# Raw k and v of three pairs of batches in 1-MB loads, and raw rows in weight buffers that are still empty: retention and a top-2 mixture of experts on one core

## The chip, the core and the metric

The kernel runs on one core of a Trainium2 chip. The metric is the device time of one execution in microseconds (us); before the change its median is 443.01 us over 3 runs (438.04, 443.01 and 443.7).

The core has five engines with a queue of instructions each, which they work off in order: PE (matmuls; PEld is its weight load, which overlaps), DVE, ACT, POOL and SP. SP only issues loads and stores (DMAs); POOL issues those that gather, scatter or convert, beside its own work. An instruction that waits holds up what stands behind it in its queue.

## What is computed

The inputs q, k and v have 8 batches, 8 heads, 576 positions and head size 64, in float32. The reference, cut:

```python
scores = (1/8) * q @ k^T
ret = scores * Dmat            # Dmat[h, i, j] = gamma_h ** (i - j) where i >= j, else 0
attn = ret @ v                 # (8, 8, 576, 64)
x = attn.transpose(0, 2, 1, 3).reshape(4608, 512)
logits = x @ w_gate + log1p(exp(x @ w_noise)) * noise    # (4608, 8)
# the two best experts of each row, softmax over the two:
out[row] += weight * (relu(x[row] @ w1[e]) @ w2[e])      # w1[e] 512 x 1024, w2[e] 1024 x 512
```

## The kernel before, in words

**Units.** The attention part handles the batches in four pairs (bp = 0 to 3). A pair has four units u = 4 bp to 4 bp + 3: its two batches, each in two halves of four heads. `unit` (L430) gives pair, half (hq) and batch of u. A unit covers the first 512 positions; the last 64 of all heads of a pair form a "tail" (`load_tail` L464, `tail` L643).

**Raw rows.** `load` (L437) brings a unit's rows to the chip: q in a tile of 128 x 1024 float32 (two loads of 256 KB, one for each pair of heads), k and v in two such tiles each (c = 0 and 1, 256 positions each). The k and v tiles hold all 8 heads of one batch, so they serve two units: units 0 and 1 load their four heads each (256 KB a load), and from unit 2 on the first unit of a batch loads both halves (512 KB a load). In a k or v load each partition gets 512 bytes per head in one piece, in a q load 2 KB. All these tiles come from a class of 10 buffers, "big", which the experts' weights use later too.

**What happens to them.** `cast` (L475) converts a unit's raw rows to bfloat16 in "half" buffers: k on ACT or DVE (L489, L491), q on POOL or DVE with a table of decays (L498), v likewise (L505). `tr` transposes k and q on PE (L527, L521), `scores` (L552) and `states` (L585) multiply, `out_` (L620, L630) writes the unit's rows, transposed, to a tile xT of the pair.

**Routing.** When a pair is done, `route` (L711) computes the gates (PE L734), the two best experts and the ranks of the rows in them (DVE and POOL, many small operations; PE L798, L800), a table of rows per expert (PE L851), and writes the rows, transposed back (PE L874), with their weights and targets, from "xg" buffers to a buffer xd in memory (SP L883).

**Experts.** A tile of an expert gathers up to 128 rows per block from xd (POOL L1007, indirect), transposes them (PE L1029), multiplies by w1 (L1083 in pairs of blocks early on, L1109 with up to four blocks later) and w2 (L1171, L1181), and stores to or adds to rows in memory (SP L1229, POOL L1203 and L1238). The early pairs of blocks, of experts 0 to 2, start while attention still runs (`CLOSE`, L34: how many rows of each expert are worked on after each pair of batches). The three weight buffers W0 to W2 (128 x 8192 bfloat16) are filled for these experts by converting loads that POOL issues (`weights`, L932; L940 and L944, four of 512 KB each as stored), the later experts' through "big" (L954, L957) and casts to W. W0 is loaded once unit 10's rows have landed, W1 and W2 once unit 15's have (`WAIT`, L31).

**The order.** `record` (L1248) lists all operations with a priority (the unit, or 100 and more for experts); a planner, `Plan.run` (L114), then walks through them with estimated costs, and picks each time what can start first on an engine, by when its inputs, a buffer of its class and the engine are free. Where two engines are given for an operation it picks one. What comes out is a fixed order of instructions for each of the five queues. So another cost, another buffer or another transfer anywhere moves instructions in all queues. Estimated landing: 0.24 us per head for a k or v load, 0.72 for a q load. There are 8 semaphores for SP's loads, so that a load waits until the eighth before it has landed.

Of the kernel before, what the change touches and what calls it, by code (L numbers as in the profile page):

```python
# [8 lines left out]
F32 = mybir.dt.float32  # L9
F16 = mybir.dt.float16  # L10
BF16 = mybir.dt.bfloat16
# [6 lines left out]
P = 128  # L18
N = 4608
NCOL = N // P  # L20
E = 8
F = 1024
DM = 512
KD = DM // P
KF = F // P
# [219 lines left out]
class Kernel:  # L245
    def __init__(self, tc, ctx, src, gates, noise, w1, w2, out, xd, yd):
        self.tc, self.nc = tc, tc.nc
        self.src, self.gates, self.noise, self.w1, self.w2, self.out = src, gates, noise, w1, w2, out
        self.xd, self.yd = xd, yd
        nc = self.nc  # L250
        self.pl = pl = Plan()
        self.cp = ctx.enter_context(tc.tile_pool(name="fix", bufs=1))
        self.ps = ctx.enter_context(tc.tile_pool(name="ps", bufs=1, space=bass.MemoryType.PSUM))
        mk = lambda n, k, sh, dt: [(self.cp.tile(sh, dt, name=f"{n}{i}"), None) for i in range(k)]
        pl.cls("big", mk("big", 10, [P, 1024], F32), exp=4, xt=3, rt=1)
        pl.cls("half", mk("half", 21, [P, 512], F32), cs=9, exp=15, xt=3, tl=6, rt=1)
# [175 lines left out]

    def inp(self, fn, t, prio, dma):

        self.inps.append(self.pl.op("SP", 0.55, fn, w=[t], prio=prio, dma=dma, after=self.inps[-5:-4]))

    def load(self, u):  # L437
        pl, nc = self.pl, self.nc
        bp, hq, b = self.unit(u)
        d = self.u[u] = {}  # L440

        if not hq:
            self.raw = {n: [pl.buf("big", "att") for c in range(2)] for n in "kv"}
        for n in "kqv":
            if n == "q":
                t = d["rawq"] = pl.buf("big", "att")
                s = self.src[n][2 * bp + b, 4 * hq:4 * hq + 4]

                for a in range(2):
                    self.inp(lambda e, s=s, t=t, a=a: nc.sync.dma_start(  # L450
                        out=t.t[a::2].rearrange("p (h x) -> p h x", h=2),
                        in_=s[2 * a:2 * a + 2, :512].rearrange("h (p r) d -> p h (r d)", r=8)), (t, a), u, 0.72)
                continue
            d["raw" + n] = self.raw[n]
            if hq and u > 1:
                continue
            h0, nh = (4 * hq, 4) if u < 2 else (0, E)
            for c, t in enumerate(self.raw[n]):
                self.inp(lambda e, n=n, t=t, c=c: nc.sync.dma_start(
                    out=t.t[:, h0 * P:(h0 + nh) * P].rearrange("p (h x) -> p h x", h=nh),  # L460
                    in_=self.src[n][2 * bp + b, h0:h0 + nh, 256 * c:256 * c + 256].rearrange("h (p r) d -> p h (r d)", r=2)),
                    (t, hq) if u < 2 else t, u, 0.24 * nh)

    def load_tail(self, bp, prio):  # L464
        pl, nc = self.pl, self.nc
        d = self.tails[bp] = {}
        for n in "kqv":
            t = d["raw" + n] = pl.buf("half", "tl")
            for b in range(2):
                self.inp(lambda e, n=n, t=t, b=b: nc.sync.dma_start(  # L470
                    out=t.t[b * HD:(b + 1) * HD].rearrange("p (h d) -> p h d", h=E),
                    in_=self.src[n][2 * bp + b, :, 512:, :].rearrange("h s d -> s h d")),
                    (t, b), prio, 0.8)

    def cast(self, u):  # L475
        pl, nc = self.pl, self.nc
        d = self.u[u]
        hq = self.unit(u)[1]
        hs = slice(4 * hq, 4 * hq + 4)
        tab, tabq = self.fixed["tab"], self.fixed["tabq"]  # L480
        bf = lambda b: b.t.bitcast(BF16)
        kn, qb, vn = (pl.buf("half", "cs") for _ in range(3))
        rk, rq, rv = d.pop("rawk"), d.pop("rawq"), d.pop("rawv")

        def k(e, c):
            i = rk[c].t.rearrange("p (g h r d) -> p g h r d", g=2, h=4, r=2)[:, hq]
            o = bf(kn).rearrange("p (r c h d) -> p c h r d", r=2, c=2, h=4)[:, c]
            if e == "ACT":
                nc.scalar.activation(o, i, Act.Copy, scale=0.125)  # L489
            elif e == "DVE":  # L490
                nc.vector.tensor_scalar_mul(o, i, 0.125)  # L491
        for c in range(2):
            pl.op({"ACT": 0.63, "DVE": 0.43}, 0, lambda e, c=c: k(e, c), r=[(rk[c], hq)], w=[(kn, c)], prio=u, port=True)

        def q(e):
            i = rq.t.rearrange("p (h r d) -> p h r d", h=2, r=8)
            o = bf(qb).rearrange("p (r h d) -> p h r d", r=8, h=2)
            self.eng(e).tensor_tensor(o, i, tabq.t[:, 2 * hq:2 * hq + 2].unsqueeze(3).to_broadcast([P, 2, 8, HD]), Alu.mult)  # L498
        pl.op({"DVE": 1.23, "POOL": 1.91} if u > 1 else {"DVE": 1.23}, 0, q, r=[rq, tabq], w=[qb], prio=u, port=True)

        def v(e, c):
            i = rv[c].t.rearrange("p (g h r d) -> p g h r d", g=2, h=4, r=2)[:, hq]
            o = bf(vn).rearrange("p (r c h d) -> p c h r d", r=2, c=2, h=4)[:, c]
            t = tab.t[:, hs, 2 * c:2 * c + 2].unsqueeze(3).to_broadcast([P, 4, 2, HD])
            self.eng(e).tensor_tensor(o, i, t, Alu.mult)  # L505
        for c in range(2):
            pl.op({"DVE": 0.69, "POOL": 1.06}, 0, lambda e, c=c: v(e, c), r=[(rv[c], hq), tab], w=[(vn, c)], prio=u, port=True)
        d.update(kn=kn, qb=qb, vn=vn)

    def tr(self, u):  # L510
# [737 lines left out]
    def record(self):  # L1248
        pl = self.pl
# [7 lines left out]
        for u in range(NU + 1):  # L1257
            bp = u // 4
# [29 lines left out]
        self.ne = ne = len([t for t in ts if t[2] < 3])  # L1288
        landed = lambda u: [o for o in pl.ops if o.dma and o.prio == u]
        for e, u in enumerate(WAIT):  # L1290
            self.weights(e, 40 + e, True, landed(u))

        ahead = 2
        fetched = 0
        for i, t in enumerate(ts[:ne]):
# [5 lines left out]
            g = self.down(i, t)  # L1301
            for k in range(KF):
                r, w, c = g.deps(k)
# [4 lines left out]
        for i in range(ne, len(ts) + 1):  # L1308
# [4 lines left out]
            if i < len(ts):  # L1313
                e = ts[i][0]
# [8 lines left out]
            else:  # L1323
                e, po, hT = ts[-1][0], self.t[i - 1]["po"], self.t[i - 1]["hT"]
                for s in range(len(po)):
                    def last(_, s=s):
# [3 lines left out]
                        else:  # L1330
# [3 lines left out]
                          r=[(hT[f // 2], f) for f in range(KF)] + [(self.W[e], KD + f) for f in range(4)], w=[po[s]], prio=pr)  # L1334
# [164 lines left out]
```

## Time and profile before

| what | us |
|---|---|
| median of three runs | 443.01 |
| span of the profiled execution, first to last instruction | 439.4 |
| PE busy | 381.7 |
| POOL busy | 282.1 |
| ACT busy | 248.1 |
| DVE busy | 181.6 |

Of the profiled execution itself the record gives the span; it lies between the lowest and the median of the three times. A line of the profile gives the line of the kernel (L505 is line 505), the engine, the operation, the tiles (written <- read, buffer numbers left out) and how often. "[2.46 <-POOL half L498]" says that the engine stood idle for 2.46 us ahead of it and that POOL's work at line 498, which wrote a "half" buffer, ended the wait. "PEclk" is the share of PE's full clock that was granted; it is 1 or 0.5 at any moment. The share of the 16 DMA engines can exceed 1, since packets overlap.

### The profile page before, as it was taken

How to read it: one execution, taken by the hardware profiler on the slowest of the kernel's cores; microseconds unless marked ns; L12 is line 12 of the kernel's file. 1: busy time of each engine (PE TensorE's matmuls, PEld its weight loads, DVE VectorE, ACT ScalarE, POOL GpSimd, SP SyncE). 2: the span in 40 equal slices, each digit the busy share in tenths (PEclk: the TensorE clock that was granted, in tenths of full speed). 3: DMA queues.
4: the chain of work that ended last, by engine and by line, in shares of the span. 5: the costliest groups of instructions: out<-in, count | busy, mean ns of one | idle time of the engine just before them, and what ended most of it. 6: DMA issues, size and time to landing. Idle time of an engine off the chain costs nothing. (4 is left out here: it accounts for less than half of the span.)

```text
span 439.4 us, 11274 instructions
## 1 busy us (share of the span) xinstructions
PE 381.7 (87%) x4352; PEld 242.1 (55%) x4352; DVE 181.6 (41%) x501; ACT 248.1 (56%) x422; POOL 282.1 (64%) x363
## 2 busy tenths in 40 slices
PE   2787676778899859999999999999999997999990
PEld 1576566667677646765566544545544543454450
DVE  4744488784378665202243452143123211222231
ACT  5688586777776646657656647464446332434320
POOL 8774788795889526553447766666676562777544
PEclk9999698679999988999999999999999998999996
DMA  8997999999996999548499996996999999765524
GB/s 244 310 263 160 303 267 262 304 277 264 277 264 108 218 211 264 169 143 278 127 354 375 362 384 192 328 339 167 311 365 133 168 147 267 202 209 189 165 75 145
DMA packets 98235, 105.36 MB, mean 240 GB/s; under 512 B 31711, under 2 KB 72160, under 8 KB 98179
## 3 DMA queue, kind: packets, MB, share of 16 engines
q1 hardware_dynamic: 82914, 67.72, 52.6%
q0 software_dynamic: 15264, 36.89, 34.3%
q8 instruction: 35, 0.57, 0.6%
q14 instruction: 22, 0.17, 0.1%
HBM read 83.20 MB, written 26.63 MB: 250 GB/s over the span
## 5 line engine op out<-in xcount | busy, mean ns | idle before, releaser
L1171 PE MATMUL ps<-W,half 128*128 128x512 bf16 x576 | 189.1, 384 | 4.8 <-ACT half L1092 2.8
L1109 PE MATMUL ps<-big,W 128*128 128x512 bf16 (+4 forms) x640 | 182.1, 330 | 0.7 <-ACT half L1092 0.7
L1092 ACT ACTIVATE half<-ps 128x512 bf16<-128x512 f32 (+5 forms) x181 | 90.3, 506 | 106.6 <-PE ps L1109 88.8
L1007 POOL DMA_INDIRECT xg<-xd,xi x80 | 84.1, 1052 | 69.3 <-issue 17.9
L1171 PEld LDWEIGHTS <-half 128*128 128x128 bf16 x576 | 56.1, 99 | 67.6 <-issue 5.2
L1109 PEld LDWEIGHTS <-W 128*128 128x128 bf16 x640 | 62.8, 98 | 47.6 <-issue 1.7
L1233 DVE SCALAR_TENSOR_TENSOR half<-ps,xg,half 128x512 f32<-128x512 f32 (+1 forms) x46 | 30.4, 667 | 68.6 <-PE ps L1171 49.1
L1238 POOL DMA_INDIRECT out_dram<-half,xg x39 | 38.8, 994 | 23.4 <-DVE half L1233 8.9
L560 DVE TENSOR_TENSOR half<-ps,mask 128x512 bf16<-128x512 f32 x64 | 40.5, 682 | 20.8 <-PE ps L552 17.7
L1203 POOL DMA_INDIRECT half<-yd,xg x39 | 39.4, 1010 | 11.9 <-issue 10.4
L279 ACT ACTIVATE half<-ps 128x1024 bf16<-128x1024 bf16 (+1 forms) x35 | 34.4, 1002 | 6.5 <-PE ps L521 2.7
L505 POOL TENSOR_TENSOR half<-big,tab 128x512 bf16<-128x512 f32 x32 | 33.5, 1060 | 3.7 <-DMA big<-in_v_dram 3.5
L1083 PE MATMUL ps<-half,W 128*128 128x256 bf16 (+1 forms) x288 | 29.6, 258 | 5.6 <-ACT xg L279 3.9
L498 POOL TENSOR_TENSOR half<-big,tabq 128x1024 bf16<-128x1024 f32 x14 | 26.6, 1902 | 8.0 <-DMA big<-in_q_dram 5.5
L1083 PEld LDWEIGHTS <-W 128*128 128x128 bf16 x288 | 24.3, 99 | 9.4 <-issue 6.4
L279 ACT ACTIVATE tb<-ps 64x512 bf16<-64x512 f32 x32 | 18.9, 591 | 18.5 <-PE ps L585 17.3
L279 ACT ACTIVATE W<-big 128x1024 bf16<-128x1024 f32 x23 | 23.9, 1052 | 7.6 <-DMA big<-in_moe_w_dram 6.8
L1233 DVE SCALAR_TENSOR_TENSOR half<-ps,gm,half 128x512 f32<-128x512 f32 x6 | 4.5, 751 | 52.9 <-ACT half L1223 29.6
L1223 ACT ACTIVATE half<-ps,xg 128x512 f32<-128x512 f32 x28 | 19.1, 685 | 9.6 <-PE ps L1171 8.5
L279 ACT ACTIVATE xT<-ps 128x512 bf16<-128x512 f32 (+1 forms) x40 | 19.9, 555 | 6.2 <-PE ps L701 4.7
L279 ACT ACTIVATE xg<-ps 128x1024 bf16<-128x1024 bf16 (+1 forms) x19 | 17.1, 934 | 7.4 <-DMA xd<-xg 7.3
L489 ACT ACTIVATE half<-big 128x512 bf16<-128x512 f32 x29 | 17.6, 633 | 5.5 <-DMA big<-in_k_dram 5.4
(189 smaller groups left out, 445.6 us busy)
## 6 DMA issues: line engine op xcount, KB each, us to landing
big<-in_moe_w_dram SPq DMA_DIRECT2D x40, 512.0 KB, 8.9
yd<-half SPq DMA_DIRECT2D x41, 256.0 KB, 7.7
big<-in_q_dram SPq DMA_DIRECT2D x32, 256.0 KB, 8.7
big<-in_k_dram SPq DMA_DIRECT2D x14, 512.0 KB, 6.3
big<-in_v_dram SPq DMA_DIRECT2D x14, 512.0 KB, 9.8
W<-in_moe_w_dram POOLq DMA_DIRECT2D x12, 512.0 KB, 9.2
xd<-xg SPq DMA_DIRECT2D x16, 264.0 KB, 6.4
xg<-xd,xi POOLq DMA_INDIRECT x80, 5.9
```

The source lines that it names most:

```text
L279: self.nc.scalar.activation(out, in_, Act.Copy)
L498: self.eng(e).tensor_tensor(o, i, tabq.t[:, 2 * hq:2 * hq + 2].unsqueeze(3).to_broadcast([P, 2, 8, HD]), Alu.mult)
L505: self.eng(e).tensor_tensor(o, i, t, Alu.mult)
L560: nc.vector.tensor_tensor(S.t.bitcast(BF16).rearrange("p (h c x) -> p h c x", h=2, c=2)[:, h], p[h].t.rearrange("p (c x) -> p c x", c=2), ...
L1007: ins = nc.gpsimd.indirect_dma_start(out=x.t[:n, :], out_offset=None, in_=self.xd[:rows, :], in_offset=IOff(ap=xi.t[:n, h:h + 1], axis=0), ...
L1083: nc.tensor.matmul(pv()[:, f2, :], lhsT=w.t[:, o:o + P], rhs=xv()[:, di, :n], start=(di == 0), stop=(di == KD - 1))
L1092: self.nc.scalar.activation(o, i, Act.Relu)
L1109: self.mm = nc.tensor.matmul(p.t[:, :n], lhsT=w.t[:, o:o + P], rhs=xv()[:, di, :n], start=(di == 0), stop=(di == KD - 1))
L1171: self.mm = self.nc.tensor.matmul(po.t, lhsT=hv[:, c:c + P], rhs=self.W[e].t[:, o:o + DM], start=(f == 0), stop=(f == KF - 1))
L1203: pl.op("POOL", 1.3, lambda _, b=b, iy=iy, n=self.size(j): nc.gpsimd.indirect_dma_start(out=b.t[:n, :], out_offset=None, in_=self.yd[:rows ...
L1233: pl.op("DVE", 0.75 if n == P else 0.86, lambda _, o=o, b=b, po=po, g=g, n=n: [nc.vector.scalar_tensor_tensor(o.t[:n, c], x, g()[:n], b.t[ ...
L1238: ins = nc.gpsimd.indirect_dma_start(out=self.out[:, :], out_offset=IOff(ap=io()[:n], axis=0), in_=o.t[:n, :], in_offset=None, bounds_chec ...
```

## The change

- Units 0 to 2: as before, 256 KB per load for units 0 and 1 and 512 KB for unit 2; but the tiles now hold both batches of the pair (16 groups of 64 columns by 2 positions, 128 x 2048 float32), so that `cast` picks one of four quarters of a tile (x4) instead of one of two halves.
- Pairs 1 to 3: k and v come once per pair, at its first unit, in two loads of 1 MB each (both batches and all heads of 256 positions).
- Where they lie: those of pairs 0 and 2 in the weight buffers W1 and W2, which hold four such tiles (class "wkv"); those of pairs 1 and 3 in "big", whose ten buffers are now five adjoining pairs.
- q of units 0 to 7 lies in W0, which holds four q tiles (class "wq"); from unit 8 on in "big".
- W0 may be loaded, beside the old condition, once all raw q in it are cast, W1 and W2 once all raw k and v in them are.
- The planner's estimate of a k or v load is 0.22 us per group of 64 columns by 2 positions instead of 0.24.

The core of the diff:

```diff
-        pl.cls("big", mk("big", 10, [P, 1024], F32), exp=4, xt=3, rt=1)
+        bs = [self.cp.tile([P, 2, 1024], F32, name=f"big{i}") for i in range(5)]
+        pl.cls("big", [(x[:, i, :], x) for x in bs for i in range(2)], exp=4, xt=3, rt=1)
...
-        pl.cls("W", mk("W", 3, [P, KD * F + KF * DM], BF16))
+        ws = [self.cp.tile([P, KD * F + KF * DM], BF16, name=f"W{i}") for i in range(3)]
+        pl.cls("W", [(x, None) for x in ws])
+        part = lambda x, i, n: x[:, 2 * i * n:2 * i * n + 2 * n].bitcast(F32)
+        pl.cls("wkv", [(part(x, i, 2048), None) for x in ws[1:] for i in range(2)])
+        pl.cls("wq", [(part(ws[0], i, 1024), None) for i in range(4)])
...
     def load(self, u):
...
-        if not hq:
-            self.raw = {n: [pl.buf("big", "att") for c in range(2)] for n in "kv"}
+        if u % 4 == 0:
+            self.raw = {n: [pl.buf("big", "att", 2) if bp % 2 else pl.buf("wkv", "att") for c in range(2)] for n in "kv"}
...
-                t = d["rawq"] = pl.buf("big", "att")
+                t = d["rawq"] = pl.buf("wq", "att") if u < 8 else pl.buf("big", "att")
...
-            if hq and u > 1:
+            if bp and u % 4 or u == 3:
                 continue
-            h0, nh = (4 * hq, 4) if u < 2 else (0, E)
+            m = slice(0, 2 * E) if bp else slice(4 * u, (4, 8, 16)[u])
             for c, t in enumerate(self.raw[n]):
-                self.inp(lambda e, n=n, t=t, c=c: nc.sync.dma_start(
-                    out=t.t[:, h0 * P:(h0 + nh) * P].rearrange("p (h x) -> p h x", h=nh),
-                    in_=self.src[n][2 * bp + b, h0:h0 + nh, 256 * c:256 * c + 256].rearrange("h (p r) d -> p h (r d)", r=2)),
-                    (t, hq) if u < 2 else t, u, 0.24 * nh)
+                w = [t] if bp else [(t, x) for x in range(m.start // 4, m.stop // 4)]
+                self.inp(lambda e, n=n, t=t, c=c, m=m, bp=bp: nc.sync.dma_start(
+                    out=rows(t, m),
+                    in_=self.src[n][2 * bp:2 * bp + 2].rearrange("b h s d -> (b h) s d")[
+                        m, 256 * c:256 * c + 256].rearrange("h (p r) d -> p h (r d)", r=2)),
+                    w, u, 0.22 * (m.stop - m.start))
...
         def k(e, c):
-            i = rk[c].t.rearrange("p (g h r d) -> p g h r d", g=2, h=4, r=2)[:, hq]
+            i = flat(rk[c]).rearrange("p (g h r d) -> p g h r d", g=4, h=4, r=2)[:, x4]
...
         for e, u in enumerate(WAIT):
-            self.weights(e, 40 + e, True, landed(u))
+            raw = (("wkv", "att"), ("wq", "att"))[e == 0]
+            self.weights(e, 40 + e, True, landed(u) + [o for b in pl.fifo[raw] for o in b.ops])
```

The casts of v and the sources of the tails change in the same way as those of k; `rows` and `flat` give the view of a tile in one piece.

More of the change, by code (lines that the diff above doesn't have):

```diff
@@ L433, in inp @@
     def inp(self, fn, t, prio, dma):
[L435 removed]
+        self.inps.append(self.pl.op("SP", 0.55, fn, w=t, prio=prio, dma=dma, after=self.inps[-5:-4]))
     def load(self, u):
@@ L492, in cast @@
         for c in range(2):
-            pl.op({"ACT": 0.63, "DVE": 0.43}, 0, lambda e, c=c: k(e, c), r=[(rk[c], hq)], w=[(kn, c)], prio=u, port=True)
+            pl.op({"ACT": 0.63, "DVE": 0.43}, 0, lambda e, c=c: k(e, c), r=[(rk[c], x4)], w=[(kn, c)], prio=u, port=True)
         def q(e):
@@ L506, in cast @@
         for c in range(2):
-            pl.op({"DVE": 0.69, "POOL": 1.06}, 0, lambda e, c=c: v(e, c), r=[(rv[c], hq), tab], w=[(vn, c)], prio=u, port=True)
+            pl.op({"DVE": 0.69, "POOL": 1.06}, 0, lambda e, c=c: v(e, c), r=[(rv[c], x4), tab], w=[(vn, c)], prio=u, port=True)
         d.update(kn=kn, qb=qb, vn=vn)
```

12 lines of the change are left out of this document (8 added, 4 removed).

## The prediction

> **What bounds the kernel now.** I read the windows first, with the span cut at the ends of its stages: 0 to 140 us holds the sixteen attention units, 140 to 175 the last two routings, and from 175 on only expert work is left. The columns are the stretch, its length, busy time (and instructions) of PE, PEld, DVE, ACT and POOL, the granted PE clock, the DMA engines' share, and GB/s.
>
> ```profile
> 0.00:45.00 45.00, 28.37 (x672) 23.85 (x672) 23.70 (x128) 31.22 (x46) 30.37 (x67) 1.00 0.92 241
> 45.00:90.00 45.00, 32.96 (x824) 28.02 (x826) 33.38 (x82) 32.20 (x56) 36.40 (x48) 0.81 1.05 285
> 90.00:140.00 50.00, 43.02 (x908) 33.98 (x901) 30.88 (x72) 37.05 (x62) 40.38 (x57) 0.93 0.99 247
> 140.00:175.00 35.00, 27.94 (x354) 20.46 (x354) 21.96 (x84) 20.19 (x37) 18.21 (x39) 0.90 1.00 216
> 175.00:439.00 264.00, 249.43 (x1608) 135.84 (x1606) 71.72 (x138) 127.39 (x224) 156.74 (x155) 0.98 0.80 234
> ```
>
> After 175 us PE is busy 249.43 of 264 us, so that part is PE's own work and the change leaves that work alone. Ahead of it PE stands idle 16.6 us (to 45), 12.0 (to 90), 7.0 (to 140) and 7.1 (to 175), 42.7 in all. The same PE work has to be done before and after, so what the change can win is a part of these 42.7 us, and a microsecond by which an attention unit comes earlier is worth a microsecond only if PE has nothing less to do in that time. In the stage that matters, 45 to 140, POOL is the busiest: 76.8 of 95 us.
>
> Next I looked at the DMA: three windows of ten microseconds, then the issues (transfers of each kind, KB each, median us from issue to landing).
>
> ```profile
> 10.00:20.00 10.00, 7.68 (x149) 6.67 (x149) 7.68 (x22) 6.01 (x10) 6.76 (x25) 1.00 1.13 314
> 30.00:40.00 10.00, 7.95 (x269) 7.04 (x261) 6.96 (x12) 9.54 (x16) 5.85 (x7) 1.00 0.90 178
> 60.00:70.00 10.00, 8.13 (x250) 6.85 (x248) 9.04 (x25) 8.15 (x15) 8.72 (x17) 1.00 0.93 224
> ```
>
> ```profile
> big<-in_q_dram SPq DMA_DIRECT2D x32, 256.0 KB, 8.7
> big<-in_k_dram SPq DMA_DIRECT2D x14, 512.0 KB, 6.3
> big<-in_v_dram SPq DMA_DIRECT2D x14, 512.0 KB, 9.8
> ...
> big<-in_v_dram SPq DMA_DIRECT2D x4, 256.0 KB, 4.3
> ```
>
> Loads run at 314 GB/s when the queue is full and fall to 178 and 224 GB/s in the two stretches in which the small tail loads are issued: 1.36 MB and 0.90 MB not moved, 7.2 us at 314 GB/s.
>
> Third, who waits for raw rows. These lines are the raw buffers' own view from 0 to 140 us: casts by engine with shortest, median and longest ns, and then the idle time of the casting engines by the kind of load that ended it.
>
> ```profile
> L505 POOL TENSOR_TENSOR half<-big,tab x32: 1037/1047/1479, 8.9 to 136.4; 128x512 bf16<-128x512 f32 x32
> L489 ACT ACTIVATE half<-big x29: 613/630/652, 4.2 to 129.2; 128x512 bf16<-128x512 f32 x29
> ...
> L498 POOL TENSOR_TENSOR half<-big,tabq x14: 1895/1902/1926, 19.8 to 130.5; 128x1024 bf16<-128x1024 f32 x14
> ...
>   DMA big<-in_q_dram: 6.9, 4
>   DMA big<-in_k_dram: 5.4, 3
>   DMA big<-in_v_dram: 3.5, 4
> ```
>
> Only 15.8 us of waiting in eleven waits, the first loads of the run among them. So the loads don't hold the casts up much directly. They do it through the order written into each queue: the planner places a cast where it expects its rows. On PE and POOL (start, duration, what, and the idle time before it) that looks so:
>
> ```profile
> 46.30 1.03 PE L521 MATMUL ps<-ident__69,half 128*128 128x128 bf16 x8 [2.46 <-POOL half L498]
> ...
> 92.56 0.51 PE L527 MATMUL ps<-ident__69,half 128*128 128x128 bf16 x6 [2.11 <-ACT half L489]
> ...
> 138.79 0.23 PE L585 MATMUL ps<-half,half 64*64 64x64 bf16 x4
> ...
> 154.63 0.59 PE L1171 MATMUL ps<-W,half 128*128 128x512 bf16 x2 [1.91 <-DMA W<-in_moe_w_dram]
> ```
>
> ```profile
> 35.20 1.05 POOL L505 TENSOR_TENSOR half<-big,tab 128x512 bf16<-128x512 f32 x1 [1.62 <-DMA big<-in_v_dram]
> ...
> 82.10 1.74 POOL L940 DMA_DIRECT2D W<-in_moe_w_dram  x2
> 86.79 1.14 POOL L1007 DMA_INDIRECT xg<-xd,xi  x1 [2.95 <-DVE scr L756]
> ...
> 94.42 1.56 POOL L1007 DMA_INDIRECT xg<-xd,xi  x1 [0.30 <-issue]
> ...
> 104.80 1.05 POOL L505 TENSOR_TENSOR half<-big,tab 128x512 bf16<-128x512 f32 x1 [1.21 <-DMA big<-in_v_dram]
> 111.27 1.11 POOL L1007 DMA_INDIRECT xg<-xd,xi  x1 [5.42 <-DVE half L560]
> ```
>
> The last states matmuls of unit 15 are at 138.79. POOL gathers (L1007) and W0's loads (L940) stand between q and v casts and hold them up.
>
> **The change part by part.** Transfers: k and v take 36 issues now (4 and 14 each); the changed kernel has 24, since each of the last three pairs takes four of 1 MB instead of eight of 512 KB. Bytes and rows of 512 B stay. At 314 GB/s with an engine share of 1.13 the engines have no gap between transfers that a merger could close, so the direct gain is 0; twelve SP issues less are hidden behind the full queue.
>
> Pairs' first units: unit 4 now needs its v behind 1 MB more of k and 1 MB more of v, 2.1 MB or 6.8 us at 314 GB/s; against that the dip to 178 GB/s is filled. Its second v cast, at 35.20, comes 2 to 7 us later, I take 4. Behind it PE waited 2.46 us for unit 5's q anyway, and q5 still follows the tails, so I count between 3 us lost and nothing. Units 6 to 8 then have their k and v at hand; POOL's 8.6 us without work from 45 to 90 bound what that gives, and I take 2. Together 1 us earlier, between 3 later and 4 earlier.
>
> Order on POOL around units 9 and 10: by the built programs W0's first two loads now stand ahead of q9, not behind v10. W0's buffer may be filled once the raw q of units 0 to 7 are cast, which is long past. That costs units 9 and 10 up to 1.74 us, and nothing from unit 11 on, whose casts stand behind these loads in both orders.
>
> Units 11 and 12: both gathers (1.14, and 1.56 after 0.30) go from ahead of unit 11's casts to between q12 and v12. Unit 11 gains their 3.0 us; from v12 on only the wait ahead of them counts, 2.95 us, of which I take half, since the routing's next small operation on POOL needs DVE too. The wait of 1.21 us at 104.80 for v12, and PE's of 2.11 us at 92.56 for a k cast, go, as those rows now lie there. For v12 and all that follows 1.5 + 1.2 = 2.7 us, bounds 0 and 4.2.
>
> Units 13 to 15: ahead of the last v cast the changed POOL has three gathers less (five for eight, 1.11 each), one weights load (0.87), one q cast (1.90) and one half of a v cast (1.05) less, 7.1 us; q13 and that half go to DVE, which is busy 30.88 of 50 us there. The wait of 5.42 us stays, since such a gather is still ahead of q14 and q15. Bounds 2 and 8, taken 7.1. Unit 15 so ends 1 + 2.7 + 7.1 = 10.8 us earlier, at 128; the bounds add up to 1 later and 16 earlier.
>
> What is given back: the planner puts less expert work into that time. Ahead of unit 15's last states the old order has 64 up (L1083) and 30 down matmuls (L1171), the new one 32 and 12.
>
> ```profile
> L1171 PE MATMUL ps<-W,half 128*128 128x512 bf16 x56 | 15.6, 415 | 1.9 <-DMA W<-in_moe_w_dram 1.9
> ...
> L1083 PE MATMUL ps<-half,W 128*128 128x256 bf16 x101 | 12.6, 272 | 1.7 <-ACT half L279 1.2 <-DVE half L281 0.5
> ```
>
> Busy time over count is 0.125 us for an up and 0.279 us for a down matmul (0 to 170 us, slow clock included): 32 x 0.125 + 18 x 0.279 = 9.0 us of PE work moves behind unit 15. PE's idle time falls by 10.8 - 9.0 = 1.8 us only. To that comes the clock: 0.93 over 90 to 140 is half speed for 7 us, begun after the wait at 92.56; without it up to 3 us of PE time, I take 1.5.
>
> Behind unit 15: up to the last table the difference shrinks to 24 up and 8 down, 5.2 us, so PE has work while the two routings run, one after the other through the same DVE tiles. W1 and W2 are loaded once their raw rows are cast and unit 15's rows have landed, which is earlier; their loads still follow the last casts on POOL. The wait of 1.91 us at 154.63 may become 0 or 4 us; I take no change.
>
> Sum: 1.8 + 1.5 = 3.3 us less, a span of 436.1 instead of 439.4. The profiled span is 3.6 us under the median of the three runs shown, 443.01 (438.04 to 443.7), so against the median I forecast 439.7, rounded to 440.
>
> A rule that speaks for much more: four k and v transfers of 256 KB landed after 4.3 us, k's of 512 KB after 6.3, so a line through both has 2.3 us that don't grow with size, and twelve transfers less would be 27 us if the queue paid them one after another. The Trainium skill, "DMA: Bandwidth & Descriptors" (Anatomy of one DMA; Bandwidth) says the same: about 2.0 us fixed per DMA, and batch to 1 MiB or more; by its figure 24 us, an estimate. The windows at 314 GB/s show the fixed part overlapped, and the same page's rules for authors have it overlap where DMAs are issued early.
>
> **Rivals.** (A) The sum above, 436 to 442 us: 0.43.
>
> (B) The loads, not POOL, space the units. Then filling the dips gives the whole 7.2 us, and units without stalls keep PE's clock up: 0.81 over 45 to 90 is half speed for 17 us, about 8 us of PE time, of which I allow 5. 443 - 12 = 431 (429 to 433). For it: the two dips. Against it: POOL's 36.4 of 45 us. 0.22.
>
> (C) Nothing moves: rows lie there earlier, and the casts still wait for their place in POOL's queue and for the `half` buffers that they write. 443 (442 to 446). For it: only 15.8 us of waits for rows. 0.18.
>
> (D) Slower. The 1-MB v of the last pair goes into buffers that hold raw q of units 8 to 11, so its second transfer can't be issued before q11 is cast (after the gather at 86.79 now), and behind it on SP stand the writes of routed rows that the gathers and so q14 wait for. With 9.8 us to landing of a 512-KB v, it decides once q11 is cast later than about 92 us; then units 12 to 15 slip by up to those 9.8 us, and the time is 453. 0.13.
>
> (E) The 2.3 us that don't grow with size are paid twelve times in series, on the path: 443 - 27 = 416. For it: the two medians. Against it: the windows at 314 GB/s. 0.04. By the figure of the Trainium skill, "DMA: Bandwidth & Descriptors", it would be 419, an estimate.
>
> **How the numbers follow.** 440 is A's. Faster by over 2% (under 434.1; 2% is about what a measurement of this kernel can tell from no change) is 0.20 of B, E and 0.02 of A: 0.26. Slower by over 2% (above 451.9) is 0.12 of D and 0.01 of C: 0.13. The rest is 0.61. A range of 429 to 450 leaves out E, the lowest 0.03 of B and 0.12 of D.
>
> **What would show it.** Right: the last L585 at 124 to 130 us instead of 139; PE idle ahead of 175 us near 40 us, more of it saved ahead of 140 than lost behind; more L1083 and L1171 behind the last states; the GB/s at 30 to 40 us well above 178. Wrong: the last L585 at 136 or later (then C or, with SP waiting on the v of unit 12, D), PE idle for over 10 us between unit 15 and the last table (then the routings are what counts), or PE idle under 33 us with the clock near 1.00 from 45 us on (then B).

## The result, and the profile after

The changed kernel takes 458.7 us (median of 4 runs, 457.62 to 464.37), the kernel before 441.95 on the same chip (4 runs, 438.04 to 443.7): a ratio of 1.056, 95% interval 1.038 to 1.074. It is slower, and outside the range of 429 to 450 us. Medians and ranges here are of all runs; ratios and their intervals leave out disturbed executions, so a ratio can differ a little from the quotient of two medians.

The profiled execution took 459.39 us, its span is 457.8. The changed kernel's lines that are named here stand 8 to 12 further down than before: loads of k and v L459 -> L468, of q L450 -> L458, of tails L470 -> L480, casts of q and v L498 and L505 -> L510 and L517, transposes L521 -> L533, states L585 -> L597, writes to xd L883 -> L895, the wide matmuls L1109 -> L1121. The changed kernel's windows by stage, in the columns of the prediction's first fence:

```profile
0.00:45.00 45.00, 25.36 (x526) 20.84 (x528) 21.91 (x118) 27.04 (x40) 27.17 (x69) 0.89 0.96 258
45.00:90.00 45.00, 29.89 (x730) 26.16 (x727) 26.48 (x56) 27.29 (x45) 30.99 (x44) 0.80 0.89 229
90.00:140.00 50.00, 34.10 (x670) 29.20 (x670) 35.43 (x67) 30.18 (x48) 29.55 (x41) 0.73 0.84 220
140.00:175.00 35.00, 31.62 (x686) 24.38 (x685) 27.00 (x87) 22.14 (x42) 26.09 (x46) 1.00 0.87 182
```

PE now idles 19.6, 15.1, 15.9 and 3.4 us in the four stages, 54.0 ahead of 175 us where it was 42.7, and between 90 and 140 the granted clock fell from 0.93 to 0.73. The loads slowed down with it, 220 GB/s there for 247. In the two windows around the first pair's tails, still of the changed kernel:

```profile
30.00:40.00 10.00, 7.00 (x176) 5.80 (x169) 3.27 (x7) 6.73 (x11) 2.75 (x2) 0.77 0.93 244
40.00:50.00 10.00, 5.98 (x124) 5.28 (x117) 3.09 (x5) 4.09 (x8) 3.90 (x7) 0.55 0.77 152
```

The dip is not gone, it has moved. Between 20 and 60 us the poorest ten microseconds of the changed kernel are those at 40 to 50, with 152 GB/s; in the kernel before they are at 32 to 42 us, with 137 GB/s:

```profile
32.00:42.00 10.00, 7.68 (x223) 6.77 (x224) 5.24 (x10) 8.65 (x14) 5.29 (x8) 1.00 0.78 137
```

SP's queue tells why. First the kernel before (start, duration, loads issued), then the changed one:

```profile
40.12 1.28 SPq L450 DMA_DIRECT2D big<-in_q_dram  x2
...
58.90 3.91 SPq L470 DMA_DIRECT2D half<-in_k_dram  x2
...
99.29 6.36 SPq L883 DMA_DIRECT2D xd<-xg  x5
...
108.82 2.21 SPq L450 DMA_DIRECT2D big<-in_q_dram  x2
```

```profile
31.38 1.06 SPq L468 DMA_DIRECT2D big<-in_v_dram  x1
...
35.05 0.71 SPq L468 DMA_DIRECT2D big<-in_v_dram  x1
35.88 2.86 SPq L480 DMA_DIRECT2D half<-in_k_dram  x1
...
47.55 1.28 SPq L458 DMA_DIRECT2D W<-in_q_dram  x2
...
69.67 4.40 SPq L480 DMA_DIRECT2D half<-in_k_dram  x2
...
114.16 2.31 SPq L480 DMA_DIRECT2D half<-in_q_dram  x1
122.95 3.39 SPq L895 DMA_DIRECT2D xd<-xg  x5
126.39 1.29 SPq L458 DMA_DIRECT2D big<-in_q_dram  x2
```

The four lines of the kernel before are unit 5's q, the first tail load of pair 1, the writes of pair 1's routed rows and, behind them, unit 13's q. In the changed kernel the same four are at 47.55, 69.67, 122.95 and 126.39: later by 7.4, 10.8, 23.7 and 17.6 us. The first step is easy to see: k and v of the pair's second batch, 2 MB that nobody needs before unit 6, now stand ahead of eleven small loads (the tails and the noise, 35.88 to 46.90 us), and behind all of them stands the q that unit 5 needs. SP comes to the first of the eleven 6.4 us later than before (35.88 for 29.50), about the time of 2.1 MB at 314 GB/s, 6.7 us. The eleven themselves, of 8 to 128 KB, take SP 11.0 us here and 10.0 us in the kernel before, about 1 us each; in both kernels the dip lies there and just behind.

What the casts wait for: POOL's timeline of the changed kernel.

```profile
34.57 1.90 POOL L510 TENSOR_TENSOR half<-W,tabq 128x1024 bf16<-128x1024 f32 x1 [5.85 <-DMA W<-in_q_dram]
39.15 1.05 POOL L517 TENSOR_TENSOR half<-big,tab 128x512 bf16<-128x512 f32 x1 [2.68 <-DMA big<-in_v_dram]
43.53 1.05 POOL L517 TENSOR_TENSOR half<-big,tab 128x512 bf16<-128x512 f32 x1 [3.33 <-DMA big<-in_v_dram]
52.10 1.90 POOL L510 TENSOR_TENSOR half<-W,tabq 128x1024 bf16<-128x1024 f32 x1 [1.85 <-DMA W<-in_q_dram]
```

Unit 4's second v cast is at 43.53 (35.20 before), unit 5's q cast at 52.10 (before, PE's wait at 46.30 ended with it). And PE:

```profile
44.63 1.20 PE L597 MATMUL ps<-half,half 128*64 128x64 bf16 x24 [3.85 <-POOL half L517]
...
94.95 0.75 PE L709 MATMUL ps<-half,half 64*64 64x64 bf16 x16 [8.13 <-DVE half L696]
...
139.15 0.62 PE L533 MATMUL ps<-ident__69,half 128*128 128x128 bf16 x8 [2.81 <-DVE half L510]
...
152.57 0.23 PE L597 MATMUL ps<-half,half 64*64 64x64 bf16 x4
...
221.12 4.14 PE L1121 MATMUL ps<-big,W 128*128 128x448 bf16 x21
...
250.54 0.32 PE L1121 MATMUL ps<-big,W 128*128 128x192 bf16 x1 [5.93 <-ACT half L1104]
```

The last states of unit 15 are at 152.57 instead of 138.79. The first wide matmul of the experts starts at 221.12; before the change it is this row:

```profile
200.97 6.38 PE L1109 MATMUL ps<-big,W 128*128 128x448 bf16 x33
```

So 20.2 us are lost ahead of it, more than the 18.4 by which the span grew. Up to unit 15 the loss grows in jumps, and a part is made up in between. The start of the q transposes of units 4, 5, 8, 9, 12, 13 and 15 is (before, after): 33.1 and 36.5, 46.3 and 54.1, 65.3 and 75.1, 77.7 and 96.0, 105.3 and 116.7, 119.0 and 139.2, 133.4 and 149.2.

The jump at unit 9 has a cause of its own, which the prediction did not foresee. A cast of 30 columns on DVE, the list of rows for the gathers, in the changed kernel's DVE timeline, and POOL's timeline of the same time:

```profile
86.10 8.47 DVE L875 CAST xi<-L 128x30 int32<-128x30 f32 x1
94.48 0.74 DVE L696 TENSOR_TENSOR half<-ps,maskt 128x256 bf16<-128x256 f32 x2
```

```profile
85.74 1.07 POOL L669 TENSOR_TENSOR half<-half,tab 128x512 bf16<-128x512 f32 x1
86.76 1.91 POOL L510 TENSOR_TENSOR half<-big,tabq 128x1024 bf16<-128x1024 f32 x1
88.61 2.04 POOL L517 TENSOR_TENSOR half<-W,tab 128x512 bf16<-128x512 f32 x2
90.62 1.89 POOL L510 TENSOR_TENSOR half<-big,tabq 128x1024 bf16<-128x1024 f32 x1
92.48 2.04 POOL L517 TENSOR_TENSOR half<-W,tab 128x512 bf16<-128x512 f32 x2
```

The cast took 8.47 us, until POOL's last cast in a row was done; in the kernel before it took 0.29. The next work in DVE's queue is what PE waited 8.13 us for at 94.95.

The jump at unit 13 has a cause on DVE, too. Its q is cast there now:

```profile
134.28 0.69 DVE L1106 TENSOR_SCALAR half<-ps 128x512 bf16<-128x512 f32 x1 [6.44 <-PE ps L1095]
134.89 4.20 DVE L510 TENSOR_TENSOR half<-big,tabq 128x1024 bf16<-128x1024 f32 x1
```

The cast stands behind a step of an early expert (L1106), for which DVE waited 6.44 us, and then takes 4.20 us beside POOL's work from 134.08 to 138.00. On DVE it took 1.21 and 1.22 us in the first units. It is what PE waits 2.81 us for at 139.15. This q was asked for at 126.39 and 127.06, and loads of its kind landed after a median of 4.4 us, so by that estimate it lay there at about 131.5: the order in DVE's queue, not the load, ended the wait.

### The profile page after: what moved, and what is told of

The parts are those of the page before. It is cut to its first block, busy times and chain, and to the rows that moved or that the text cites. A ratio compares the mean times of both kernels' runs of the same rounds, so it can differ in the third digit from the quotient of the medians.

```text
span 457.8 us, 11254 instructions
## 1 busy us (share of the span) xinstructions
PE 387.2 (85%) x4352; PEld 248.3 (54%) x4352; DVE 193.4 (42%) x499; ACT 246.3 (54%) x420; POOL 279.8 (61%) x367
## 5 line engine op out<-in xcount | busy, mean ns | idle before, releaser
L1121 PE MATMUL ps<-big,W 128*128 128x512 bf16 (+4 forms) x640 | 181.6, 330 | 5.9 <-ACT half L1104 5.9
L1104 ACT ACTIVATE half<-ps 128x512 bf16<-128x512 f32 (+5 forms) x181 | 89.3, 498 | 109.3 <-PE ps L1121 97.4
L1121 PEld LDWEIGHTS <-W 128*128 128x128 bf16 x640 | 62.9, 98 | 47.8 <-issue 0.9
L284 ACT ACTIVATE half<-ps 128x1024 bf16<-128x1024 bf16 (+1 forms) x31 | 31.1, 1015 | 14.3 <-PE ps L533 5.0
L1235 ACT ACTIVATE half<-ps,xg 128x512 f32<-128x512 f32 x32 | 21.9, 684 | 16.5 <-PE ps L1183 16.4
L284 ACT ACTIVATE W<-big 128x1024 bf16<-128x1024 f32 x22 | 22.3, 1051 | 7.7 <-DMA big<-in_moe_w_dram 7.5
L597 PE MATMUL ps<-half,half 64*64 64x64 bf16 (+2 forms) x512 | 20.0, 231 | 7.0 <-POOL half L517 3.8
L533 PE MATMUL ps<-ident__69,half 128*128 128x128 bf16 x128 | 13.3, 266 | 12.5 <-POOL half L510 4.7
L597 PEld LDWEIGHTS <-half 64*64 64x64 bf16 (+1 forms) x512 | 17.2, 125 | 10.4 <-issue 8.4
L564 PE MATMUL ps<-half,half 64*64 64x128 bf16 x512 | 13.5, 256 | 9.4 <-ACT half L284 8.5
```

The source lines that it names most:

```text
L284: self.nc.scalar.activation(out, in_, Act.Copy)
L597: nc.tensor.matmul(o[h * HD:(h + 1) * HD, hp, n, :], lhsT=kk[:k, r, c, y], rhs=vv[:k, r, c, y].unsqueeze(1).to_broadcast([k, n.stop - n.st ...
L1104: self.nc.scalar.activation(o, i, Act.Relu)
L1121: self.mm = nc.tensor.matmul(p.t[:, :n], lhsT=w.t[:, o:o + P], rhs=xv()[:, di, :n], start=(di == 0), stop=(di == KD - 1))
L1235: nc.scalar.activation(y.t[:n, c], x, Act.Copy, scale=g()[:n])
```

## The experiments

Sixteen runs were made, in four groups, each group on one chip with runs of the kernel before. In the first group the kernel before itself took 463.74 us, so its times are compared within the group only; the changed kernel was not run there. A dash means that the record has no ratio. One thing limits all of these but e2: an edit to the loads or the estimate makes the planner order all queues anew, so that none of them changes SP's queue alone. POOL's order, for one, differs from the changed kernel's from 45 us on in e8 and from 60 us on in e5.

| run | what it is | us, median (range) | before, there | ratio and interval |
|---|---|---|---|---|
| e1 | after, k and v in 512 KB, batch by batch | 450.75 (447.01-455.24) | 463.74 (456.35-469.48) | - |
| e2 | after, one cast reads PSUM | 475.98 (470.47-478.05) | same | 1.032 (0.996-1.068) |
| e3 | after, estimate 0.30 | 473.37 (467.02-477.44) | same | 1.025 (0.989-1.060) |
| e4 | before, estimate 0.22 | 452.86 (445.34-456.74) | same | 0.987 (0.951-1.024) |
| c_after | after | 458.35 (452.24-462.9) | 442.33 (438.0-444.84) | 1.038 (1.030-1.047) |
| e5 | after's place, 512 KB | 457.68 (451.01-463.12) | same | - |
| e6 | pair 1 as in e1, pairs 2 and 3 in 1 MB | 446.84 (442.56-450.51) | same | 1.009 (1.003-1.014) |
| e7 | pair 1 in 1 MB, the others as in e1 | 463.84 (456.18-467.16) | same | - |
| e8 | after, tails of pair 0 behind q5 | 448.32 (448.0-451.49) | 443.07 (439.43-447.69) | 1.013 (1.005-1.020) |
| e9 | before, tails of pair 0 behind q5 | 441.16 (436.07-442.81) | same | 0.988 (0.978-0.997) |
| e10 | e1 again | 433.64 (432.21-443.5) | same | 0.978 (0.972-0.983) |
| e11 | e1, tails of pair 0 behind q5 | 447.2 (438.42-451.86) | same | 0.996 (0.989-1.002) |
| e12 | e1, estimate 0.24 | 440.96 (433.51-447.45) | 443.18 (431.74-445.65) | - |
| e13 | e1 again | 433.85 (430.58-435.0) | same | - |
| e14 | e4 again | 441.27 (439.62-443.22) | same | - |
| e15 | after | 454.88 (453.11-455.32) | same | - |

**The joint loads undone, everything else kept (e1, e10, e13), and the whole change beside it (e15).** The edit to the changed kernel; every load of k or v is then 512 KB or less and is asked for with the first unit of its own batch:

```diff
-            if bp and u % 4 or u == 3:
+            if u % 2 and u > 1:
                 continue
-            m = slice(0, 2 * E) if bp else slice(4 * u, (4, 8, 16)[u])
+            m = slice(4 * (u % 4), 4 * (u % 4) + (8 if u > 1 else 4))
             for c, t in enumerate(self.raw[n]):
-                w = [t] if bp else [(t, x) for x in range(m.start // 4, m.stop // 4)]
+                w = [(t, x) for x in range(m.start // 4, m.stop // 4)]
```

> The changed kernel with all its new buffers, but k and v of the last three pairs in 512-KB loads, one batch at a time, as before the change. Theory 1 (the 1-MB loads make the first unit of a pair wait, and that lag is the loss): 441 to 447 us, unit 4's second v cast back near 35 us. Theory 2 (the loss is made where DVE and POOL get in each other's way once the order has slipped, the 8.47-us cast of xi above all): 447 to 453. Theory 3 (each new estimate reshuffles the order, and any reshuffle of this order costs): anywhere from 445 to 460.

> The changed kernel's buffers and estimate with all k and v loads batch by batch in 512-KB pieces, again, on another chip (there 450.75 us beside 463.74 of the kernel before). Theory C: at most 445 us, since no early rows stand ahead of q5; if the buffers (raw rows in weight buffers) are worth something by themselves, 434 to 440; if the first chip's lead was that chip's noise, 440 to 445.

> e10 again (buffers and the new estimate of 0.22, 512-KB loads batch by batch), as the reference for the other three on this chip: 432 to 437 us, PE's first wide matmul at 193 to 199.

> The whole change on the same chip: 452 to 463 us. Theory (the joint loads cost more than the whole difference): 20 to 28 us above e13. Rival (buffers and joint loads don't add, e13 is a lucky order): e13 at 440 or more, and the whole change 12 to 18 us above it.

On the last chip e13 took 433.85 us and the whole change 454.88: 21.0 us between them, and the ranges don't touch. Against the kernel before, e10 is faster (0.978, interval 0.972 to 0.983); e13's median is 9.3 us lower on another chip, where one run of the kernel before also came to 431.74. So the joint loads, with the order that comes with them, cost more than the whole difference, and the rest of the change pays a part of it back. Unit 4's second v cast is back at 35.30 in e1 and 35.99 in e13. The SP queue of e13 and then of e15:

```profile
40.72 1.29 SPq L458 DMA_DIRECT2D W<-in_q_dram  x2
...
59.53 3.92 SPq L480 DMA_DIRECT2D half<-in_k_dram  x2
...
101.24 4.57 SPq L895 DMA_DIRECT2D xd<-xg  x5
...
110.90 1.30 SPq L458 DMA_DIRECT2D big<-in_q_dram  x2
```

```profile
47.50 1.28 SPq L458 DMA_DIRECT2D W<-in_q_dram  x2
...
66.92 4.35 SPq L480 DMA_DIRECT2D half<-in_k_dram  x2
...
120.61 3.11 SPq L895 DMA_DIRECT2D xd<-xg  x5
...
123.77 1.72 SPq L458 DMA_DIRECT2D big<-in_q_dram  x2
```

These are the same four entries as above; with the 512-KB loads they are back at the places of the kernel before, within 2.1 us. And the first wide matmul on PE, of e13 and then of e15:

```profile
197.71 6.38 PE L1121 MATMUL ps<-big,W 128*128 128x448 bf16 x33
```

```profile
216.78 6.38 PE L1121 MATMUL ps<-big,W 128*128 128x448 bf16 x33
```

Of the 21.0 us, 19.1 lie ahead of it.

**Size or place (e5).** Both batches are asked for at the pair's first unit, as in the changed kernel, but in 512-KB loads:

```diff
-            m = slice(0, 2 * E) if bp else slice(4 * u, (4, 8, 16)[u])
-            for c, t in enumerate(self.raw[n]):
-                w = [t] if bp else [(t, x) for x in range(m.start // 4, m.stop // 4)]
+            ms = [slice(0, E), slice(E, 2 * E)] if bp else [slice(4 * u, (4, 8, 16)[u])]
+            for m, c, t in [(m, c, t) for m in ms for c, t in enumerate(self.raw[n])]:
+                w = [(t, x) for x in range(m.start // 4, m.stop // 4)]
```

> The changed kernel, with k and v of both batches still asked for at the pair's first unit, but in twice as many loads of 512 KB, the first batch's ahead of the second's. Theory A (the size: the first unit has to wait for a whole 1-MB load): unit 5's transposes of q at 46 to 48 us, the first wide matmul at 199 to 206. Theory B (the place: the second batch's rows stand in SP's queue ahead of the tails and of the next q): unit 5 at 52 to 56 us as in the changed kernel, the first wide matmul at 214 to 222.

457.68 us beside 458.35 of the changed kernel on the same chip. For unit 5 the place decides: its q transposes start at 54.08 (52.83 in c_after), as Theory B has it, although unit 4's second v is cast 4.0 us earlier than in the changed kernel's first profile:

```profile
39.55 1.05 POOL L517 TENSOR_TENSOR half<-big,tab 128x512 bf16<-128x512 f32 x1 [1.07 <-DMA big<-in_v_dram]
```

The equal medians are two different sums, though. The first wide matmul comes at 206.50 (215.76 in c_after), in neither theory's range, and the cast of the list of rows takes 2.52 us instead of 8.46. From there to the end of PE's work it is 234.1 us instead of 226.8. So it is not shown that the size as such is worth nothing. A large part of the lead is given back in one wait, for an activation that stands in ACT's queue behind casts of weights, which wait for their loads:

```profile
237.01 0.32 PE L1121 MATMUL ps<-big,W 128*128 128x192 bf16 x1 [7.01 <-ACT half L1104]
```

**Which pair (e6, e7).** e6 asks for pair 1 as e1 does and for pairs 2 and 3 in 1 MB; e7 the other way round:

```diff
-            if bp and u % 4 or u == 3:
+            if (u % 2 and u > 1) if bp < 2 else u % 4:
...
-            m = slice(0, 2 * E) if bp else slice(4 * u, (4, 8, 16)[u])
+            m = slice(4 * (u % 4), 4 * (u % 4) + (8 if u > 1 else 4)) if bp < 2 else slice(0, 2 * E)
```

```diff
-            if bp and u % 4 or u == 3:
+            if (u % 2 and u > 1) if bp != 1 else u % 4:
...
-            m = slice(0, 2 * E) if bp else slice(4 * u, (4, 8, 16)[u])
+            m = slice(4 * (u % 4), 4 * (u % 4) + (8 if u > 1 else 4)) if bp != 1 else slice(0, 2 * E)
```

> The changed kernel, but pair 1 loads k and v batch by batch in 512 KB, at its first and third unit; pairs 2 and 3 keep their 1-MB loads. Theory C (the lag made at unit 5 is passed on and is the whole loss): the first wide matmul at 199 to 206 us. Theory D (each pair adds a lag of its own): 206 to 215. If the later pairs make the whole loss: 216 to 222.

> The mirror: only pair 1 has 1-MB loads, pairs 2 and 3 load batch by batch in 512 KB. Theory C: the first wide matmul at 216 to 222 us. Theory D: 206 to 215. If pair 1's lag is made up later: 199 to 206.

The first wide matmul comes at 204.73 in e6, where Theory C put it, but at 212.68 in e7, where Theory D put it; no theory has both. Pair 1's joint loads alone (e7) make the kernel as slow as all three pairs', or slower: 463.84. Without them (e6) 446.84 remain. Against the kernel before, that looks like "pair 1 is the whole loss". Against e10 and e13, the right base, it isn't: pairs 2 and 3 cost about 13 us by themselves (446.84 to 433.64 and 433.85; other chips, on which the kernel before took 443.07 and 443.18 beside 442.33 here). The parts don't add up, 30 and 13 against 21 to 25 together. And e7 loses its time elsewhere: its unit 5 starts at 55.67, but its unit 15 at 135.06, close to the 133.43 of the kernel before, so the units' lag is made up. Its first wide matmul still comes 15.0 us later than e13's, and from there to the end of PE's work it takes 236.7 us, e13 225.9. That is another order of the experts' work, not a late unit, and how the loss splits by pairs stays open. In SP's queue pairs 2 and 3 act in the same way, one pair later, as e6's SP queue shows:

```profile
65.52 5.22 SPq L480 DMA_DIRECT2D half<-in_k_dram  x2
...
107.68 5.80 SPq L895 DMA_DIRECT2D xd<-xg  x5
...
115.80 1.95 SPq L458 DMA_DIRECT2D big<-in_q_dram  x2
```

The tails of pair 1 stand 6.0 us later than in e13, behind pair 2's second batch; the writes of pair 1's routed rows 6.4 later, and unit 13's q 4.9 later.

**The small loads moved out of q5's way (e8, e9, e11).** The six tail loads of pair 0 are recorded one unit later and below q5 in priority; in e8 with the changed kernel, in e9 with the one before, in e11 with e1:

```diff
-            if u < NU and u % 4 == 1:
-                self.load_tail(bp, u + 1.5)
+            if u < NU and u % 4 == (2 if u < 4 else 1):
+                self.load_tail(bp, 5.2 if u < 4 else u + 1.5)
```

> The changed kernel with the six tail loads of pair 0 asked for one unit later, so that both halves of q5 stand ahead of them in SP's queue, directly behind the 1-MB v of pair 1 and five small noise loads; bytes and sizes are the same. Theory C in its finer form (what costs the time is that q5 stands behind 2 MB more AND behind the small loads, which are now asked for behind them): q5 is asked for at 36 to 39 us instead of 47.5, unit 5's q transposes start at 45 to 49 instead of 54.1, the routing of pair 0 follows its tails (last tail load near 47, as in the changed kernel), and the time is 443 to 451. Rival F (unit 4's own late v, 8 us, is enough, and q5's place adds nothing): unit 5 stays at 52 or later and the time at 454 to 461.

> The kernel before with the same shift of the six tail loads of pair 0 behind q5. Before, PE waited 2.46 us for q5's cast at 46.30. If q5's place is what spaces units 5 and on, unit 5's q transposes start at 41 to 44 us and the time is 437 to 441; if units 5 to 8 are held by the casts' own pace on POOL, the start moves by under 2 us and the time stays at 441 to 445. Either way it says how much of a gain in e8 belongs to the shift itself and not to the changed kernel.

> e10 with the six tail loads of pair 0 behind q5 as in e8. If the two shifts add, 432 to 439 us, and this is the version that beats both kernels; if POOL's pace hides them, 439 to 445. The start of unit 5's q transposes: 41 to 45 us.

e8: the 1-MB loads are all there, and the loss falls to 5.3 us (448.32 against 443.07); the whole change lost 16.8, 16.0 and 11.7 us in its three comparisons (458.7, 458.35 and 454.88 against the kernel before beside them). q5's two loads are asked for at 38.38 and 41.00 instead of 47.55, unit 5's q transposes start at 47.31 instead of 54.06:

```profile
47.31 0.93 PE L533 MATMUL ps<-ident__69,half 128*128 128x128 bf16 x8
```

Unit 4's second v is still cast late here:

```profile
42.65 1.05 POOL L517 TENSOR_TENSOR half<-big,tab 128x512 bf16<-128x512 f32 x1 [2.96 <-DMA big<-in_v_dram]
```

With e5 this settles unit 5: an early v and a late q5 left it late, a late v and an early q5 brought it forward. Rival F (unit 4's own late v is enough) expected 454 to 461, and falls. How much of the loss hangs on q5's place is less clear. Against the kernel before, more than half of the loss is gone. Against e10 on the same chip, which has no joint loads, 14.7 us remain, where e15 and e13 are 21.0 apart: about a third is gone. And e8 changes more than q5: pair 0's routed rows are written at 75.06 instead of 97.28, and the cast of its list of rows takes 0.18 us instead of 8.47. The shift by itself is worth little: e9 has unit 5 at 40.8 instead of 46.3, but unit 6 at 53.4 (53.1 before), and 441.16 us against 443.07, an interval that reaches to 0.997. In e11 the two shifts did not add, against the expectation: unit 5 comes at 39.7, unit 6 at 52.2 (53.3 in e1), and pair 0's ranks, for which the tails are needed, at 65.7 (62.9); 447.2 us, 13.6 more than e10 on the same chip. In e9 and e11 an early unit 5 brought little or nothing, as unit 6 didn't follow. The loss of e11, whose loads are those of e10 in another order, also shows what a new order of the queues can cost. e8 and e11 differ by the joint loads and the order that comes with them; by their ratios, 1.013 and 0.996, these cost about 7.5 us there, with q5 ahead of the small loads in both.

**The cast that stood still (e2).** One instruction of the changed kernel: pair 0's list of rows is cast straight from PSUM. All queues stay as they are.

```diff
-        o("DVE", 0.2, lambda e: V.tensor_copy(xi.t, L.t[:, :xi.t.shape[1]]), [L], [xi])
+        if bp == 0:
+            pl.op("DVE", 0.2, lambda e: V.tensor_copy(xi.t, pT.t[:, :xi.t.shape[1]]), r=[pT, L], w=[xi], prio=prio, port=True)
+        else:
+            o("DVE", 0.2, lambda e: V.tensor_copy(xi.t, L.t[:, :xi.t.shape[1]]), [L], [xi])
```

> The changed kernel with one instruction changed: the first pair's xi is cast straight out of PSUM instead of from the copy of the same numbers in SBUF; the order of all queues stays as it is. Theory 2: the cast takes 0.3 us instead of 8.47 beside POOL's four casts, PE's wait of 8.13 us ahead of the tail goes, and the time falls by 6 to 10 us, to 449 to 453. Theory 1: the late rows set the pace anyway, 456 to 459. Theory 3 says nothing of it.

The same cast in e2's DVE timeline, beside the same row of POOL work (85.23 to 94.02):

```profile
85.58 0.18 DVE L876 CAST xi<-ps 128x30 int32<-128x30 f32 x1
```

0.18 us instead of 8.47: the length was a collision with POOL over SBUF, not work. Unit 9's transposes start at 88.2 instead of 96.0. But the lead is down to 1.9 us by the tables of pair 1 (121.0, in the changed kernel 122.9), and the first wide matmul comes at 218.13, within the 215.76 to 221.12 of three profiles of the changed kernel. The time is undecided (the interval against the kernel before is 0.996 to 1.068) and missed the expected 449 to 453, on a chip where the kernel before took 463.74. So the collision explains the jump at unit 9, and no loss of time is shown to hang on it.

**The planner's estimate (e3, e4, e12, e14).** The only edit is the constant: 0.30 in the changed kernel (e3), 0.22 in the kernel before (e4 and e14), 0.24 in e1 (e12).

```diff
-                    w, u, 0.22 * (m.stop - m.start))
+                    w, u, 0.30 * (m.stop - m.start))
```

> The changed kernel with the planner's estimate of a k or v load at 0.30 us per group instead of 0.22, so that it expects the rows later and orders the casts behind them. Theory 1: 455 to 460, since the loads are as large as before. Theory 2: open, it depends on which operations meet. Theory 3, in the form that the order was made for rows that come too early: 443 to 452.

> The kernel before the change with only the planner's estimate changed from 0.24 to 0.22 us per head, as the change has it. Theories 1 and 2: 440 to 445 us. Theory 3 (a reshuffle alone costs): 447 to 456.

> The changed kernel's buffers (raw rows in idle weight buffers, pair tiles) with 512-KB loads batch by batch and the old estimate of 0.24 a head: the buffer part of the change alone. If the buffers give the gain of e10, 431 to 437 us; if the estimate gives it, 440 to 445.

> The kernel before with the estimate of 0.22 alone, again. If the estimate gives the gain, 431 to 437; if the buffers give it, 440 to 445.

A longer estimate brings the changed kernel nothing that can be told (1.025 of the kernel before, interval 0.989 to 1.060; no expectation held on that chip; its first wide matmul is at 214.9). e4 is undecided too (0.987, interval 0.951 to 1.024). On the last chip the estimate alone gives 441.27 and the buffers alone 440.96, beside 443.18 before; both together (e13) 433.85. By the medians neither part alone carries the gain of 9 us, but e12's four runs spread from 433.51 to 447.45 and the kernel before's from 431.74 to 445.65, so that this is not shown.

**The whole change again (c_after)** stood beside e5 to e7:

> The changed kernel once more, beside the others on the same chip. All theories: over 10 us slower than the kernel before in the part up to the first wide expert matmul, which came at 221 us against 201 before, and unit 5's transposes of q at about 54 us against 46.

It gave 458.35, as the first measurement did; unit 5 started at 52.83 and the first wide matmul at 215.76.

## Why the prediction was wrong

**The step that failed** is "Pairs' first units: ... Together 1 us earlier, between 3 later and 4 earlier". It had the right row and the wrong reading in three places. Unit 4's second v cast came 8.3 us later (43.53 against 35.20), where 4 of a range of 2 to 7 was taken. "against that the dip to 178 GB/s is filled" is wrong: the dip goes with the small loads, and those were not removed but pushed behind 2 MB; it moved by 8 us, with 152 GB/s in its poorest ten microseconds for 137 before. And "q5 still follows the tails, so I count between 3 us lost and nothing" saw the queue and forgot that the tails themselves come later: unit 5 starts 7.8 us later. From there units 6 to 8, said to gain 2, lose 6.1 to 9.9. e8 and e5 show the step: with q5 ahead of the tails and all 1-MB loads in place unit 5 starts at 47.31; with q5 behind them and unit 4's v early it starts at 54.08. Of the 20.2 us lost ahead of the first wide matmul this step is 7.8. That the rest comes with the joint loads too, and with the order of the queues that they bring, e13 and e15 show; by which path it comes is in part argued.

**What followed from it.** Units 11 and 12 (2.7 earlier) and 13 to 15 (10.8 earlier in all) were costed with POOL's order alone, as if the routing in between kept its time. The queues read like a chain: a late tail, a late routing, the writes of the routed rows in SP's queue ahead of unit 13's q, and that q goes out at 126.39 instead of 108.82. No run tests the links apart, and by the estimate above the last one did not bind: unit 13's cast on DVE, which the prediction moved there without a price, stood in DVE's queue until 134.89 and took 4.20 us. Unit 15 ends 13.8 later, not 10.8 earlier. The 7.1 us less of POOL work were no use, since POOL was no longer the bound: 29.55 of 50 us between 90 and 140, where it was 40.38. The work moved behind unit 15 was costed for a gain that didn't come.

**The clock** was to give 1.5 us. With more waits there was less of it: between 90 and 140 us PE stood idle 15.9 us instead of 7.0 and was granted 0.73 instead of 0.93, and PE's busy time over the whole run is 387.2 us instead of 381.7, 5.5 more for the same matmuls.

**What held.** No direct gain of the merging shows: at the same place, the kernel takes the same time with 512 KB and 1 MB (e5), though by different sums. Rival E, 2.3 us saved per transfer, has nothing for it; its line went through a v of 256 KB (4.3 us) and a k of 512 KB (6.3), and with the 512-KB v's own 9.8 us no such fixed part is left. "Behind unit 15: ... I take no change" holds roughly: from the first wide matmul to the end of PE's work 227.0 us before and 228.6 after, of which a wait of 5.93 us at 250.54 is new (2.85 at 369.59 before).

**The rivals.** B had the dips as a gain to be had; the first only moved. C fell. D (0.13) had the sign, an SP queue, and with 453 us the nearest time, but another place: it put the delay at the last pair's v. Its condition was met, as q11 is cast at 105.62 on POOL, but the first casts of that v, at 123.41 and 124.55 on POOL, wait for no DMA. The changed kernel's SP queue shows that v out of the way, a tail load at 114.16 for 2.31 us, and then SP waiting until 122.95 for the routed rows themselves, 6.5 us, with unit 13's q behind. The loss was 17 us and began two pairs earlier, at 35 us.

**What no part of the prediction named** is the gain of the rest of the change, 9 us with 512-KB loads (e10, e13). Where it comes from is not settled: e13's attention ends no earlier than before (unit 15's q transposes at 134.3, 133.4 before), its first wide matmul comes 3.3 us earlier, and the part behind is shorter too. Buffers and estimate together gave a faster kernel on both chips. The version that beats both kernels is e10 (433.64 us, 0.978 of before, interval 0.972 to 0.983): the new buffers and the new estimate, without the joint loads.

## What to carry to other kernels

A larger load is also an earlier load for half of its bytes: before merging two, list what stands between the two places in the queue, and charge each of these the whole transfer time of the part that is moved ahead. A dip in bandwidth that belongs to small loads is moved, not filled, by putting bytes ahead of them. And measure the parts of a change apart, each against the version that differs by that part alone: here one part gave 9 us and the other cost over 20, and e8 looked like half of a cure against the kernel before and like a third against e10.

## What the runs showed of the hardware

A cast of 128 x 30 on DVE from SBUF to SBUF took 8.47 us (8.46 in c_after, 8.22 in e15) beside seven POOL instructions without a gap, 0.29 us before, and 0.18 us when it read PSUM. The Trainium skill, "SBUF — State Buffer" (Who interferes with whom), says that such a cast can take both of DVE's ports, that DVE and GpSimd share one pair under an exclusive lock, and that the one that comes second blocks. The trace agrees, and adds that DVE did not get in between POOL's instructions in a row: its cast ended only when the last of them was done.

The cast of q on DVE, which reads two tiles in SBUF, took 4.20 us beside a row of POOL instructions (4.84 in c_after, 4.77 in e15), and 1.21 us in e8.
